# Sums by heads on quarters of the array, partial sums for z, constants made on chip, and the last units in halves

## The chip, the cores and the metric

The kernel runs on one core of a Trainium2 chip. The metric is the device time of one execution in microseconds. Below, PE is TensorE (the 128x128 matmul array), DVE is VectorE, ACT is ScalarE, POOL is GpSimd and SP is SyncE, whose queue issues every DMA of this kernel.

## What is computed

A linear attention with a quadratic feature map, followed by a feed-forward net with a depthwise convolution of three taps and a gate. Batch is 4, heads 4, sequence 1088, head size 32, r is 8, d_ff is 1024.

```python
def phi(x):
    a = np.einsum('rd,bhsd->bhsr', S1, x)
    b = np.einsum('rd,bhsd->bhsr', S2, x)
    return np.einsum('bhsi,bhsj->bhsij', a, b).reshape(*x.shape[:-1], r * r)
q_p, k_p = phi(q), phi(k)
kv = np.einsum('bhsf,bhsd->bhfd', k_p, v)
z = np.sum(k_p, axis=2)
num = np.einsum('bhsf,bhfd->bhsd', q_p, kv)
den = np.einsum('bhsf,bhf->bhs', q_p, z)[..., None] + 1e-06
x = num / den                       # then heads side by side: B, S, 128
...
h = np.maximum(x @ w_in, 0.0)
conv_out = sum(conv_w[k] * hp[:, k:k + S, :] for k in range(3))   # hp: h with a zero row at both ends
gate = 1.0 / (1.0 + np.exp(-conv_out))
out = (h * gate) @ w_out
```

## The kernel before

**Small matrices.** S1, S2, the taps, w_in and w_out come as float64 and are turned into float32 on chip from their two 32-bit words (`to_f32`, steps low, e, m, clamp, f, power, sign, value). `sab` holds S1 and S2 of all four heads as a block diagonal, 64 columns. A further load `pk` (80 KB, tile `pks`) brings the 128x128 identity that every transpose needs, and `zmask`, the block mask of z. `s2t` transposes the S2 half of `sab`.

**Attention, k side**, for each batch b, in three groups g of three chunks of 128 positions. `k_ab` multiplies k by `sab` (a and b of all heads in 64 columns), `k_take` copies them to SBUF, `k_phi` makes the outer products (256 columns: 4 heads by 64 features) on DVE or POOL by `kphi`. `k_kv` sums v by features over nine chunks; it works with two heads a matmul: two matmuls of 64 array columns each, at array columns 0 and 64, both with 128 moving columns, of which only the blocks of the own head are used (`k_kvmask`). With "J" in `kvs` the nine chunks are summed in one go, with "S" group by group. `k_kvt` transposes the sum, `k_kvtake` copies it. For z the kernel doesn't sum features: `k_z` sums b times a over the positions as a 32x32 matrix on array columns 0 to 31, `k_zmask` keeps the blocks, and `k_wz` folds it with S2 into 32 extra columns of the weights by which q is multiplied (`k_wq`).

**Attention, q side**, for each batch and group: `q_ab` (a, b and the part for the denominator, 96 columns), `q_take`, `q_ac`, `q_sum`, `q_rec`, `q_div` (the quotient is taken into a). Then one of two ways by `qside`: with "T", `q_phi` makes the outer product, six PE transposes (`q_t`) turn it and ACT copies it (`q_ttake`); with "M", `q_turn` transposes the small a and b on DVE, `q_out` writes them to DRAM with four DMAs, `q_in` reads them back as repeated rows with six, and `q_phi` multiplies the rows (on DVE or POOL by `qphi`). `q_x` multiplies by the sums of batch b, on two halves of the array, and `q_hi` and `q_lo` store x as a rounded part and a rest.

**Feed-forward.** The positions of all batches stand in one row, cut into nine segments (382, seven of 510, and 404 columns). A unit is a segment and one of eight blocks of 128 hidden channels, 72 in all. Its steps are `f_in` (three matmul passes: rounded weights and rests), `f_relu` on ACT, `f_mid` (the middle tap, on ACT or DVE by `mid`), two taps on DVE, `f_gate` (sigmoid, ACT), `f_mul` on POOL (on DVE for the last unit, `late`), and `f_out` (two passes of a float32 matmul, summed over eight units in one PSUM bank). Then `f_store` (DVE) and `f_send` (DMA).

**The order of the work.** Nothing in the kernel loops in this order. `graph` lists all steps with a cost, what they wait for, the PSUM banks and buffers they hold, and a key; `schedule` plays them against models of the engines and returns one order in which every engine's queue is filled. The keys come from `CFG` (`F0`, `P`, `kdue`, `kstep`, `kvlag`, `qlead`, ...), and `loads` is the order of the input DMAs. PSUM has eight banks: four for f_in ("u"), one for the output sums ("o") and three for all the rest ("t"); a "t" step may also take a free "u" bank until the time `share`. Matmuls on a constant tile (`fill`, L512) stand in early gaps of PE.

The lines that the prediction speaks of: L512 `fill`, L592 `wqs`, L599 `s2t`, L612 `outer`, L628 `k_ab`, L646 `k_z`, L667 `k_kv`, L724 `q_turn`, L752 `q_phi` by rows, L766 `q_t`, L777 `q_x`, L825 to L827 `f_in`, L844 `f_mid` on DVE, L848 taps, L856 `f_gate`, L863 `f_mul`, L887 `f_out`, L892 `f_store`.

Of the kernel before, what the change touches and what calls it, by code (L numbers as in the profile page):

```python
# [9 lines left out]
F32 = mybir.dt.float32  # L10
# [9 lines left out]
P = 128  # L20
# [26 lines left out]
C_ID = 0  # L47
C_ZM = C_ID + P
C_END = C_ZM + HR

# [12 lines left out]
    "loads": "s k0.2 t k0.0 q0.1 k0.1 q0.0 c i1 q0.2 i0 o0 v0 i3 k1 o2 o1 k2 i2 v1 o3 v2 q2 v3 q3 k3 q1",  # L63

    "F0": 108819.35,
    "P": 2174.27,
    "wlead": -80468.59,
    "outlag": 5.18,
    "tapa": 6055.15,
    "tkey": -87094.92,  # L70

    "kdue": [59700.0, -192994.0, -123572.0, 87470.0],
    "kstep": [-4098.0, 47885.0, -31405.0, 47192.0],
    "kvlag": -40175.81,

    "qlead": [[-31940.0, 61515.0, -68231.0], [131916.0, 73634.0, 73287.0], [35879.0, -31506.0, 43322.0], [4524.0, -170059.0, -45604.0]],
# [9 lines left out]
    "stick": -20253.84,  # L86
# [12 lines left out]
ALT = {"qside": "TM", "kvs": "SJ", "fr": "FR", "mid": "AD"}  # L99
POOLS = {"u": 4, "o": 1, "t": 3, "h": 6, "s": 3, "g": 6, "f": 3, "w": 3, "kab": 6, "kp": 8, "qs": 3, "gh": 3, "os": 2, "kv": 2, "qr": 2, "qf": 2, "d": 2}  # L100
BEGIN = {"PE": 5900.0, "ACT": 3000.0, "DVE": 1800.0, "POOL": 1400.0, "SP": 29500.0}
KB = {"s": 64, "t": 25, "c": 82, "k": 557, "v": 590, "q": 557, "i": 262, "o": 262}
# [5 lines left out]
COLD = 6400.0  # L108
# [32 lines left out]

def cut(n, i, half):
    return (0, n) if not half else (0, n // 2) if i == 0 else (n // 2, n)


def graph(cfg):
# [14 lines left out]
    issue, done = 730.0, 0.0  # L161
    for name in cfg["loads"].split():
        kb = KB[name[0]] / (NG if "." in name else 1)
        issue += 430
        before, done = done, max(issue + 1400, done) + kb / (0.242 if done < 10800 else 0.413)
        landed["dma", name] = done + 60
# [14 lines left out]
    ev("wqs", c_pool(B * W_S, 1.0), [("s", "value")], key=-4e4)  # L181
    ev("s2t", c_pe(60), [("s", "value"), ("dma", "c")], [("s2ps", "t")], key=-4e4)
# [34 lines left out]
    for b in range(B):  # L217
        due, ks, lag = cfg["kdue"][b], cfg["kstep"][b], cfg["kvlag"]
        for g in range(NG):
# [5 lines left out]
            if cfg["kvs"][0][b] == "J":  # L225
                if g == NG - 1:
                    kps = [("kp", b, i) for i in range(NG)]
                    deps = [x for i in range(NG) for x in (("k_phi", b, i), dma("v", b, i))]
                    ev(("k_kv", b, g), c_pe(NG * 654 + 152, 75), deps, [(kv, "t")], [kv, *kps], key + lag)
                continue  # L230
            ev(
                ("k_kv", b, g),
                c_pe(806, 75),
# [7 lines left out]
        ev(("k_z", b), c_pe(685, 65), [("k_take", b, g) for g in range(NG)], [(("zps", b), "t")], abs_, key)  # L241
        ev(("k_zmask", b), c_dve(32), [("k_z", b), ("dma", "c")], uses=[("zps", b)], key=key)
# [6 lines left out]
        for g in range(NG):  # L249
# [28 lines left out]
            ev(("q_x", b, g), c_pe(1.667 * NT[g] + 156, 70), deps, [(x, "t")], uses, key)  # L278
            ev(("q_hi", b, g), c_act(NT[g]), [("q_x", b, g)], uses=[x], key=key)
            ev(("q_lo", b, g), c_dve(NT[g]), [("q_hi", b, g)], uses=[x], key=key)  # L280

    for u in range(NU):
# [3 lines left out]
        a, o = ("a", u), ("o", s)  # L286
# [7 lines left out]
        ev(("f_in", u), c_pe(3 * (n + 2) / 2.4 + 62, 225), [*x, ("i", j, "rest")], [(a, "u")], key=key)  # L294
        half = u >= NU - cfg["halves"]
        out, prior = key + cfg["outlag"] * step, [("f_out", u - 1, i) for i in parts(cfg, u - 1)] if u else []
        for i in parts(cfg, u):
            new = i == 0
            m = cut(n, i, half)
            m = m[1] - m[0]  # L300
            ev(("f_relu", u, i), c_act(m + 2), [("f_in", u)], [(("h", u), "h")] if new else [], [a, ("h", u)], soon)
            deps = [("f_relu", u, k) for k in range(i + 1)] + [("t", "value")]
            mid = c_act(m, 1) if cfg["mid"][s][f] == "A" else c_dve(m, 1)
            ev(("f_mid", u, i), mid, deps, uses=[a, ("h", u)], key=soon)
            ev(("f_tapa", u, i), c_dve(m, 1), [("f_mid", u, i)], uses=[a, ("h", u)], key=soon + cfg["tapa"])
            ev(("f_tapb", u, i), c_dve(m, 1), [("f_tapa", u, i)], uses=[a, ("h", u)], key=soon)
            ev(("f_gate", u, i), c_act(m), [("f_tapb", u, i)], [(("s", u), "s")] if new else [], [a, ("s", u)], soon)
            mul = c_dve(m, lock=True) if u >= NU - cfg["late"] else c_pool(m)
            ev(("f_mul", u, i), mul, [("f_gate", u, i)], [(("g", u), "g")] if new else [], [("h", u), ("s", u), ("g", u)], soon)
            first = [] if f or i else [(o, "o")]  # L310
            if cfg["fr"][s][f] == "R":
                ev(("f_high", u, i), c_act(m), [("f_mul", u, i)], [(("gh", u), "gh")] if new else [], [("g", u), ("gh", u)], soon)
                ev(("f_low", u, i), c_pool(m), [("f_high", u, i)], uses=[("g", u), ("gh", u)], key=soon)
                deps = [("f_low", u, i), ("o", j, "rest"), *prior]
                ev(("f_out", u, i), c_pe(3 * m / 2.4 + 62, 225), deps, first, [o, ("g", u), ("gh", u)], out)
            else:
                deps = [("f_mul", u, i), ("o", j, "value"), *prior]
                ev(("f_out", u, i), c_pe(4 * m / 2.4 + 5, 160), deps, first, [o, ("g", u)], out)
            if f == NF - 1:
                ev(("f_store", s, i), c_dve(m), [("f_out", u, i)], [(("os", s, i), "os")], [o], soon)  # L320
                ev(("f_send", s, i), c_dma(1, 1400), [("f_store", s, i)], uses=[("os", s, i)], key=soon)
# [3 lines left out]
def schedule(cfg):  # L325
# [11 lines left out]
    def pool(kind):  # L337
        if kind == "t" and now["PE"] < cfg["share"] and pools["u"] and pools["u"][0] < (pools["t"] or [(1e9, 0)])[0]:
            return pools["u"]
        return pools[kind]  # L340
    after = collections.defaultdict(list)
# [25 lines left out]
    for _ in range(len(events)):  # L367
        best = None
        for e in ("PE", "ACT", "DVE", "POOL", "SP"):
            able = []  # L370
            for name in waiting[e]:
                cost, _, alloc, key = events[name]
                t = max(now[e], ready[name])
                if not all(pool(kind_of[b]) for b in alloc):
                    continue
                for b in alloc:
                    t = max(t, pool(kind_of[b])[0][0])
# [10 lines left out]
        for b in alloc:  # L388
            slot[b] = heapq.heappop(pool(kind_of[b]))[1]
# [21 lines left out]
def body(ctx: ExitStack, tc: tile.TileContext, qT, kT, v, pk, ps, pt, w_in, w_out, outT):  # L411
# [41 lines left out]
    ptr = const.tile([P, 2 * W_T], I32, name="ptr")  # L453
    pks = const.tile([P, C_END], F32, name="pks")
    for name in CFG["loads"].split():
# [6 lines left out]
            "c": lambda: e.dma_start(pks, pk),  # L462
# [7 lines left out]
    ident = pks[:, C_ID : C_ID + P]  # L470
    kmask = const.tile([P, P], F32, name="kmask")
    zmask = pks[:HR, C_ZM : C_ZM + HR]
    sab = const.tile([P, W_S], F32, name="sab")
    pts = const.tile([P, W_T], F32, name="pts")
    s2b = const.tile([HR, P], F32, name="s2b")
# [93 lines left out]
    to_f32(("t",), pts, ptr, True)  # L569
# [21 lines left out]
    def wqs():  # L591
        nc.gpsimd.tensor_copy(wq[:, :, : 2 * HR], sab.unsqueeze(1).broadcast_to([P, B, 2 * HR]))  # L592
# [8 lines left out]
    def s2take():  # L601
        nc.scalar.copy(s2b, do["s2ps"][:HR, :P])
# [360 lines left out]
```

## Time and profile before

| | |
|---|---|
| median of 3 runs | 165.84 us (165.67 to 166.76) |
| the profiled execution | 166.0 us |
| its span | 164.2 us |
| PE busy | 156.4 us (95%), 823 matmuls |
| DVE busy | 147.0 us (89%) |
| ACT busy | 133.7 us (81%) |
| POOL busy | 123.2 us (75%) |
| granted PE clock | 1.00 in every slice |
| DMA | 20.34 MB, mean 124 GB/s |

The span runs from the first to the last instruction of the program; the execution's own time is a little longer. Busy times are unions of the instructions' durations on an engine. A matmul's duration holds its drain, which overlaps with the matmuls that follow, so the mean duration of one is longer than what it adds to the queue; that is read from the distance of starts. "Idle before" is the time that an engine stood still ahead of an instruction, and the releaser is what ended it.

### The profile page before, as it was taken

To read this page: it belongs to the slowest core of one execution; us is meant where nothing else is said; L and a number is where in the kernel's file an instruction comes from. 1 tells how busy PE (TensorE), PEld (TensorE's weight loads), DVE (VectorE), ACT (ScalarE), POOL (GpSimd) and SP (SyncE) were. 2 spreads that over 40 slices of the span, in tenths; PEclk is the share of its full clock that TensorE was granted. 3 is DMA by queue.
4 is the path that set the end of the run, shared out by engine and by line. 5 is a ranking of instruction groups with operands and counts; after the bars stand their busy time and mean duration, and the time that the engine had idled before them with its cause. 6 is when DMAs were issued, how large, how long until landed. Compare 5 with 4: busy or idle time off the path is not lost.

```text
span 164.2 us, 2830 instructions
## 1 busy us (share of the span) xinstructions
PE 156.4 (95%) x823; PEld 102.9 (63%) x823; DVE 147.0 (89%) x304; ACT 133.7 (81%) x284; POOL 123.2 (75%) x120
## 2 busy tenths in 40 slices
PE   7699999999999999999999999999999999999981
PEld 7588989888766756446444654664565556556620
DVE  4469999889897999999999999999999999999971
ACT  4133755649897999998998999999899998999950
POOL 3403999933997699697996769998877787779760
PEclk9999999999999999999999999999999999999999
DMA  4999999024644643545544453300100100200101
GB/s 105 264 281 411 409 411 346 23 69 106 175 97 140 198 116 98 152 140 164 158 115 133 129 168 119 115 0 0 64 0 0 68 0 0 67 2 0 64 0 50
DMA packets 19711, 20.34 MB, mean 124 GB/s; under 512 B 9712, under 2 KB 17392, under 8 KB 19696
## 3 DMA queue, kind: packets, MB, share of 16 engines
q1 hardware_dynamic: 19696, 20.17, 38.8%
q8 instruction: 6, 0.10, 0.3%
q14 instruction: 9, 0.07, 0.1%
HBM read 16.95 MB, written 3.21 MB: 123 GB/s over the span
## 4 chain that ended last, share of the span: by engine, by line
PE 74%; DMA 17%; SPq 3%; issue 2%; POOL 1%; POOLq 1%; DVE 0%
PE o L887 34%; DMA kt<-in_kT 12%; PE a L825 10%; PE a L826 9%; PE a L827 9%; PE t L777 5%; PE t L694 4%; DMA qt<-in_qT 3%; DMA w_out_raw<-d 2%; POOL g L863 1%; PE t L667 1%; PE t L628 1%; SPq L463 1%; POOLq L930 1%; SPq L464 1%
## 5 line engine op out<-in xcount | busy, mean ns | idle before, releaser
L863 POOL TENSOR_TENSOR g<-h,s 128x510 f32<-128x510 f32 (+2 forms) x71 | 87.2, 1246 | 20.0 <-ACT s L856 18.9
L848 DVE SCALAR_TENSOR_TENSOR a<-h,pts,a 128x510 f32<-128x510 f32 (+2 forms) x144 | 98.6, 720 | 4.0 <-ACT a L842 2.5
L887 PE MATMUL o<-g,w_out_sb 128*128 128x510 f32 (+2 forms) x144 | 70.7, 577 | 0.6 <-POOL g L863 0.6
L825 PE MATMUL a<-xhi,whi 128*128 128x512 f32 (+2 forms) x72 | 48.9, 679 | 0.0
L842 ACT ACTIVATE a<-h,pts 128x510 f32<-128x510 f32 (+2 forms) x67 | 45.0, 676 | 0.6
L836 ACT ACTIVATE h<-a 128x512 f32<-128x512 f32 (+2 forms) x72 | 41.5, 578 | 3.7 <-PE a L827 3.3
L856 ACT ACTIVATE s<-a 128x510 f32<-128x510 f32 (+2 forms) x72 | 41.6, 579 | 1.5 <-DVE a L848 1.4
L887 PEld LDWEIGHTS o<-g,w_out_sb 128*128 128x128 f32 x144 | 26.0, 189 | 12.0 <-POOL g L863 4.8
L826 PE MATMUL a<-xhi,wlo 128*128 128x512 f32 (+2 forms) x72 | 27.7, 384 | 0.0
L827 PE MATMUL a<-xlo,whi 128*128 128x512 f32 (+2 forms) x72 | 27.6, 384 | 0.0
L825 PEld LDWEIGHTS a<-xhi,whi 128*128 128x128 f32 x72 | 13.6, 189 | 17.8 <-ACT s L856 6.2
L826 PEld LDWEIGHTS a<-xhi,wlo 128*128 128x128 f32 x72 | 13.7, 190 | 11.4 <-issue 10.2
L827 PEld LDWEIGHTS a<-xlo,whi 128*128 128x128 f32 x72 | 13.5, 188 | 2.4
L612 POOL TENSOR_TENSOR kp<-kab 128x768 f32<-128x768 f32 x8 | 11.9, 1512 | 4.0 <-ACT kab L632 4.0
L632 ACT COPY kab<-t 128x192 f32<-128x192 f32 x12 | 3.8, 319 | 7.8 <-PE t L628 7.7
L694 PEld LDWEIGHTS t<-wq,qt 128*128 128x128 f32 x72 | 8.9, 191 | 1.5 <-ACT qab L698 0.6
L628 PE MATMUL t<-sab,kt 128*128 128x64 f32 x72 | 9.2, 274 | 0.6 <-DMA kt<-in_kT 0.6
L628 PEld LDWEIGHTS t<-sab,kt 128*128 128x128 f32 x72 | 8.7, 192 | 1.2 <-ACT f L526 0.5
L694 PE MATMUL t<-wq,qt 128*128 128x96 f32 x72 | 9.2, 275 | 0.0
L667 PE MATMUL t<-kp,vt 128*64 128x128 f32 x144 | 8.5, 275 | 0.4 <-DMA vt<-in_v 0.4
L667 PEld LDWEIGHTS t<-kp,vt 128*64 128x64 f32 x144 | 7.8, 137 | 1.0 <-DMA vt<-in_v 0.6
L612 DVE TENSOR_TENSOR kp<-kab,t 128x768 f32<-128x768 f32 x4 | 3.8, 954 | 4.0 <-ACT kab L632 4.0
(86 smaller groups left out, 142.5 us busy)
## 6 DMA issues: line engine op xcount, KB each, us to landing
vt<-in_v SPq DMA_DIRECT2D x4, 576.0 KB
w_in_raw<-d SPq DMA_DIRECT2D x10, 192.0 KB
w_in_raw<-d SPq DMA_DIRECT2D x20, 96.0 KB
w_out_raw<-d SPq DMA_DIRECT2D x10, 192.0 KB
w_out_raw<-d SPq DMA_DIRECT2D x20, 96.0 KB
kt<-in_kT SPq DMA_DIRECT2D x3, 544.0 KB
qt<-in_qT SPq DMA_DIRECT2D x3, 544.0 KB
w_in_raw<-in_w_in SPq DMA_DIRECT2D x4, 256.0 KB
```

The costliest lines, as they stand in the source:

```text
L628: nc.tensor.matmul(pv[:, :, j, :], kt[:, b, c * P : (c + 1) * P], sab, start=True, stop=True)
L667: nc.tensor.matmul(ps[64 * pr : 64 * (pr + 1), :P], vt[:, b, c, 64 * pr : 64 * (pr + 1)], st["kp", g][:, j, P * pr : P * (pr + 1)], start= ...
L694: nc.tensor.matmul(pv[:, :, j, :], qt[:, b, c * P : (c + 1) * P], wq[:, b], start=True, stop=True)
L825: nc.tensor.matmul(a[:, : n + 2], whi[:, w], xhi[:, x], start=True, stop=False)
L826: nc.tensor.matmul(a[:, : n + 2], wlo[:, w], xhi[:, x], start=False, stop=False)
L827: nc.tensor.matmul(a[:, : n + 2], whi[:, w], xlo[:, x], start=False, stop=True)
L836: nc.scalar.activation(st["h"][:, c], a[:, c], AF.Relu)
L842: nc.scalar.activation(st["a"][:, lo:hi], h, AF.Copy, scale=cw[:, f, 1:2])
L848: nc.vector.scalar_tensor_tensor(out=a, in0=h[:, lo + k : hi + k], scalar=cw[:, f, k : k + 1], in1=a, op0=ALU.mult, op1=ALU.add)
L856: nc.scalar.activation(st["s"][:, c], st["a"][:, c], AF.Sigmoid)
L863: e.tensor_tensor(out=st["g"][:, lo:hi], in0=st["h"][:, lo + 1 : hi + 1], in1=st["s"][:, lo:hi], op=ALU.mult)
L887: nc.tensor.matmul(o, w_out_sb[:, w], st["g"][:, c], start=first, stop=final)
```

## The change

- `k_kv` takes one head a matmul: four matmuls of 32 array columns a chunk, at array columns 0, 32, 64 and 96, with the 64 moving columns of the own head. `k_kvmask` reads the same 64 columns twice and masks as before. Batches 1 and 3 are summed group by group ("S"), 0 and 2 in one go.
- `k_z` puts chunk c on the quarter c % 4, so that four partial sums stand below each other; `k_zmask` works on 128 partitions, and `k_wz` sums them, since S2 now stands four times below itself (`s24`, copied on POOL in `wqs`, and a full 128x128 transpose in `s2t`, which waits for `wqs`).
- The load `pk` is gone. POOL makes the identity with a memset and an `affine_select`; `zmask` comes with the taps.
- The last three units are worked in halves of 202 columns from `f_in` on, the second half's in a bank of its own, and the output of the last segment is summed, stored and sent in two halves with a bank each.
- `q_x` may be done for two groups at once (`xs`: batches 0 and 2 groups 0 and 1, batch 1 groups 1 and 2, batch 3 one by one).
- `q_in` has four row buffers in place of two.
- `schedule` has other costs and keys, and the order of all work is drawn up anew from them. Among the choices: loads of batch 0's k in one piece and of batch 1's k ahead of batch 0's v; `mid` has nine units on DVE in place of five; the `q_phi` by rows are all on POOL (three were on DVE); batch 1's group 0 takes the way "T" in place of "M"; `kphi` has four on DVE as before, one in each batch.

```diff
-    "loads": "s k0.2 t k0.0 q0.1 k0.1 q0.0 c i1 q0.2 i0 o0 v0 i3 k1 o2 o1 k2 i2 v1 o3 v2 q2 v3 q3 k3 q1",
+    "loads": "s k0 q0.0 t q0.1 i0 k1 q0.2 v0 o1 k2 o0 i2 i1 v1 o2 o3 q2 q1 v2 i3 v3 k3 q3",
...
-    "kphi": ["DDP", "PPP", "PDP", "DPP"],
-    "qphi": ["DPP", "PPD", "PDP", "DPP"],
+    "kphi": ["PPD", "PPD", "PPD", "PPD"],
+    "qphi": ["DPP", "PPP", "PPP", "PPP"],
-    "qside": ["TTM", "MMM", "MMM", "MMM"],
-    "kvs": ["JJJJ"],
+    "qside": ["TTM", "TMM", "MMM", "MMM"],
+    "kvs": ["JSJS"],
+    "xs": ["QPQS"],
...
-    "mid": ["AAAAAAAA", "AAAAAAAA", "AAAAADAA", "AAAAAAAA", "AAAAAAAA", "AADAADAA", "AADAAAAA", "ADAAAAAA", "AAAAAAAA"],
+    "mid": ["AAAAAAAA", "DAAAAAAA", "AAAAAADA", "ADAAAAAD", "AAADAAAD", "AADAAAAA", "AADAAAAA", "AAAAAAAA", "ADAAAAAA"],
-    "halves": 0,
+    "halves": 3,
-    "share": 74099.86,
+    "share": 160744.4,
...
+GROUPS = {"S": [[0], [1], [2]], "J": [[0, 1, 2]], "P": [[0], [1, 2]], "Q": [[0, 1], [2]]}
...
+        nc.gpsimd.memset(ident, 0.0)
+        nc.gpsimd.affine_select(ident, ident, [[-1, P]], ALU.not_equal, 1.0, base=0, channel_multiplier=1)
...
     def wqs():
+        nc.gpsimd.tensor_copy(s24.rearrange("p (t r) -> p t r", r=HR), sab[:, HR:].unsqueeze(1).broadcast_to([P, P // HR, HR]))
         nc.gpsimd.tensor_copy(wq[:, :, : 2 * HR], sab.unsqueeze(1).broadcast_to([P, B, 2 * HR]))
...
-        nc.tensor.transpose(ps[:HR, :P], sab[:, HR:], ident)
+        nc.tensor.transpose(ps[:, :P], s24, ident)
...
-                nc.tensor.matmul(ps[:HR, :HR], ab[:, 1, j, :], ab[:, 0, j, :], start=c == 0, stop=c == NCH - 1)
+                t = HR * (c % 4)
+                o = ps[t : t + HR, :HR]
+                nc.tensor.matmul(o, ab[:, 1, j, :], ab[:, 0, j, :], start=c < 4, stop=c + 4 >= NCH, tile_position=(0, t))
...
-                for pr in range(2):
+                for h in range(H):
                     nc.tensor.matmul(
-                        ps[64 * pr : 64 * (pr + 1), :P],
-                        vt[:, b, c, 64 * pr : 64 * (pr + 1)],
-                        st["kp", g][:, j, P * pr : P * (pr + 1)],
+                        ps[D * h : D * (h + 1), :RR],
+                        vt[:, b, c, D * h : D * (h + 1)],
+                        st["kp", g][:, j, RR * h : RR * (h + 1)],
                         start=c == 0,
                         stop=c == NCH - 1,
-                        tile_position=(0, 64 * pr),
+                        tile_position=(0, D * h),
                     )
...
-            nc.vector.tensor_tensor(out=kvm, in0=st["kvps"][:, :P], in1=kmask, op=ALU.mult)
+            a, b = (x.rearrange("p (h r) -> p h r", h=2) for x in (kvm, kmask))
+            nc.vector.tensor_tensor(out=a, in0=st["kvps"][:, :RR].unsqueeze(1).broadcast_to([P, 2, RR]), in1=b, op=ALU.mult)
...
-        def q_x(g):
+        def q_x(last):
+            for g in next(x for x in GROUPS[CFG["xs"][0][b]] if last in x):
+                x_of(g)
...
+        half, split = len(parts(CFG, u)) > 1, len(outs(CFG, u)) > 1
+
+        def f_in(i):
+            st["a", i] = a = bank(("a", u, i), "t" if i else "u", "a")
+            lo, hi = cut(n, i, half)
+            c, w = slice(lo + 2 * i, hi + 2), slice(f * P, (f + 1) * P)
+            x = slice(OFF[g] + lo + 2 * i, OFF[g] + hi + 2)
+            nc.tensor.matmul(a[:, c], whi[:, w], xhi[:, x], start=True, stop=False)
+            nc.tensor.matmul(a[:, c], wlo[:, w], xhi[:, x], start=False, stop=False)
+            nc.tensor.matmul(a[:, c], whi[:, w], xlo[:, x], start=False, stop=True)
...
         def f_out(i):
-            c, w = slice(*cut(n, i, half)), slice(f * P, (f + 1) * P)
-            if f == 0 and i == 0:
-                acc[g] = bank(("o", g), "o", "o")
-            o, first, final = acc[g][:, c], f == 0, f == NF - 1 and i == parts(CFG, u)[-1]
+            c, w = slice(*cut(n, i, split)), slice(f * P, (f + 1) * P)
+            if f == 0:
+                acc[g, i] = bank(("o", g, i), "t" if i else "o", "o")
+            o, first, final = acc[g, i][:, c], f == 0, f == NF - 1
```

More of the change, by code (lines that the diff above doesn't have):

```diff
@@ L92 @@
     "late": 1,
-    "halves": 0,
+    "halves": 3,
     "fills": 22000.0,
-    "share": 74099.86,
+    "share": 160744.4,
 }
[L99 to L102, printed above, removed]
+ALT = {"qside": "TM", "kvs": "SJ", "fr": "FR", "mid": "AD", "xs": "SJPQ"}
@@ L139, in parts, with outs @@
     return range(2 if u >= NU - cfg["halves"] else 1)
+def outs(cfg, u):
+    return range(2 if cfg["halves"] and u >= NU - NF else 1)
 def cut(n, i, half):
@@ L293, in graph @@
         j = f * P // CVT
-        ev(("f_in", u), c_pe(3 * (n + 2) / 2.4 + 62, 225), [*x, ("i", j, "rest")], [(a, "u")], key=key)
-        half = u >= NU - cfg["halves"]
-        out, prior = key + cfg["outlag"] * step, [("f_out", u - 1, i) for i in parts(cfg, u - 1)] if u else []
+        half = len(parts(cfg, u)) > 1
+        h, g, gate, gh = ("h", u), ("g", u), ("s", u), ("gh", u)
         for i in parts(cfg, u):
-            new = i == 0
-            m = cut(n, i, half)
+            m, a = cut(n, i, half), ("a", u, i)
@@ L303, in graph @@
             mid = c_act(m, 1) if cfg["mid"][s][f] == "A" else c_dve(m, 1)
[L304 to L307, printed above, removed]
+            ev(("f_mid", u, i), mid, deps, uses=[a, h], key=soon + i)
@@ L310, in graph @@
-            first = [] if f or i else [(o, "o")]
+            ev(("f_mul", u, i), mul, [("f_gate", u, i), *[("f_mul", u, k) for k in range(i)]], [] if i else [(g, "g")], [h, gate, g], soon + i)
             if cfg["fr"][s][f] == "R":
[L312 to L315, printed above, removed]
-            else:
-                deps = [("f_mul", u, i), ("o", j, "value"), *prior]
-                ev(("f_out", u, i), c_pe(4 * m / 2.4 + 5, 160), deps, first, [o, ("g", u)], out)
+                ev(("f_high", u, i), c_act(m), [("f_mul", u, i), *[("f_high", u, k) for k in range(i)]], [] if i else [(gh, "gh")], [g, gh], soon + i)
+                ev(("f_low", u, i), c_pool(m), [("f_high", u, i)], uses=[g, gh], key=soon + i)
```

183 lines of the change are left out of this document (110 added, 73 removed).

## The prediction

> **What bounds the kernel now.** I read the split of the span into stretches first, which says which engine never rests where. Its columns are the stretch in us, its length, then the busy us and the instructions of PE, PEld (weight loads), DVE, ACT and POOL, the granted clock, the DMA share and GB/s.
>
> ```profile
> 4.90:14.24 9.34, 7.05 (x67) 6.23 (x66) 5.38 (x15) 3.56 (x13) 1.51 (x1) 1.00 0.94 296
> 14.24:155.20 140.96, 140.44 (x725) 91.19 (x726) 134.67 (x266) 125.31 (x263) 116.41 (x95) 1.00 0.37 118
> 155.20:164.20 9.00, 4.95 (x13) 1.60 (x11) 4.27 (x7) 2.87 (x7) 3.32 (x4) 1.00 0.06 23
> 60.00:150.00 90.00, 89.83 (x298) 50.69 (x297) 87.90 (x140) 86.36 (x165) 75.75 (x59) 1.00 0.26 79
> ```
>
> TensorE (PE) works 140.44 of the 140.96 us between 14.24 and 155.20: this stretch is as long as its list of matmuls. Ahead of it lies a start with 2.29 us of PE idle, behind it a tail of 9.00 us. DVE is close behind, at 134.67 of 140.96 (95.5%), and 97.7% from 60 to 150 (87.90 of 90); it will matter as soon as PE has less to do.
>
> The chain of waits (start, us, what), in the middle of the feed-forward units, says what a visit to a tiled array costs:
>
> ```profile
> 59.59 0.85 PE o L887 x2
> 60.44 0.80 PE t L777 x4
> 61.24 0.43 PE a L825
> ...
> 62.14 0.85 PE o L887 x2
> 62.99 0.24 PE a L825
> ```
>
> Two passes of 510 columns take 0.85, so 0.833 ns a column. q_x (L777) streams 384 columns in two passes on two halves at once, 0.64 by that rate, but takes 0.80, and the next f_in starts with 0.43 in place of 0.24: about 0.35 us for going there and back.
>
> **The sums by heads.** All of k_kv (L667) and two batches of k_z (L646) in the timeline (start, us, engine, line):
>
> ```profile
> 14.24 2.19 PE L667 MATMUL t<-kp,vt 128*64 128x128 f32 x36 [0.40 <-DMA vt<-in_v]
> 24.86 4.15 PE L667 MATMUL t<-kp,vt 128*64 128x128 f32 x72
> 39.13 2.19 PE L667 MATMUL t<-kp,vt 128*64 128x128 f32 x36
> 21.33 1.33 PE L646 MATMUL t<-kab 128*32 128x32 f32 x36
> ```
>
> and one batch of k_kv in slices of 10 ns (the count is of matmuls in flight, then of weight loads):
>
> ```profile
> 14.72:14.73 0.01, 0.01 (x5) 0.01 (x2) 1.00 2.10 845
> 14.73:14.74 0.01, 0.01 (x6) 0.01 (x4) 1.00 1.05 410
> 14.83:14.84 0.01, 0.01 (x5) 0.01 (x3) 1.00 2.10 819
> 14.84:14.85 0.01, 0.01 (x6) 0.01 (x4) 1.00 0.00 0
> ```
>
> In neighbouring slices two matmuls and two weight loads start, one for each half, and the next pair 0.11 us later. The step is 128 columns at 0.833 (0.107) and 3 ns. So tiles of different columns run beside each other, loads included; 18 pair-steps of 0.11 make 1.98 us a batch. Now four quarters start together and stream 64 columns: a step of 0.053 + 0.003, 18 of them, 1.01. That is 0.97 less a batch, 3.9 us in four, if four tiles do what two do. k_z goes from one tile to four: now 1.33/36, at most 37 ns an instruction and in the run about 31 (its last one's drain aside); on four tiles, between 7 or so (the offset that slices of 10 ns allow) and 31. I take 8, as the nearest row is that of the tiles that start together: 18 times 23 ns is 0.41 a batch, 1.25 us for the three batches that lie in the full stretch. The other end for both is no gain, or a loss, and is a rival below.
>
> **What is put back on PE.** The new split of k_kv in batches 1 and 3 into three pieces adds four visits, the joined q_x of batches 0, 1 and 2 take three away: between 3 x 0.35 saved and 1 x 0.35 lost, as pieces may stand beside other tiled work; I take 0.3 saved. Group 0 of batch 1 no longer goes through DRAM but through six transposes:
>
> ```profile
> 18.54 0.82 PE L766 MATMUL t<-pks,kp 128*128 128x128 f32 x6
> L752 DVE TENSOR_TENSOR w_out_raw<-w_out_raw 128x768 f32<-128x768 f32 x2 | 1.9, 952 | 0.0
> L752 DVE TENSOR_TENSOR w_in_raw<-w_in_raw 128x768 f32<-128x768 f32 x1 | 1.1, 1131 | 0.0
> L724 DVE STREAM_TRANSPOSE qr<-qab 128x192 f32<-128x192 f32 x10 | 3.7, 371 | 0.0
> L844 DVE TENSOR_SCALAR a<-h,pts 128x510 f32<-128x510 f32 x5 | 3.7, 747 | 0.0
> L752 POOL TENSOR_TENSOR w_in_raw<-w_in_raw 128x768 f32<-128x768 f32 x4 | 7.3, 1831 | 0.0
> PEld o L887 <- POOL g L863: 4.8, 8, 0.9
> ```
>
> That is +0.7 (0.82 less the overlap with what follows). PE in the full stretch: -3.9 - 1.25 - 0.3 + 0.7 = -4.75, so 136.2 of 140.96.
>
> **What holds next: DVE.** The three q_phi rows leave DVE (1.9 + 1.1), one q_turn goes (0.37), and four more f_mid come to it (4 x 0.747 = 2.99): 134.67 - 3.37 + 2.99 = 134.3. At the 97.7% that it reaches from 60 to 150 with PE full beside it, 134.3 us of work need 137.4. So I take 3.5 us off the stretch, not 4.75. ACT loses the four f_mid and gains two copies; at 125.31 it isn't near. POOL takes three q_phi of 1.83 (5.5 us): 116.41 + 5.5 is 122 of 137, 89%. Each stands ahead of the f_mul queued behind it, for which f_out on PE waits. I cost this at nothing, because g has six buffers and f_out comes some five units after its f_in, which hides it; with that cover gone, PE waits up to 0.9 each (the longest wait for POOL in the last row), 2.7 us.
>
> The group that turns to transposes also takes its ten DMAs (four out, six in) out of SP's queue, and two more qf buffers let later q_in start sooner; PE has no gap worth naming in the full stretch in which it would wait for rows (0.52 in all), so both count nothing.
>
> **The start.** In the timeline of PE, and of POOL, with two rows of the DMA issues:
>
> ```profile
> 8.46 0.28 PE L599 MATMUL t<-pks,sab 128*32 128x128 f32 x1 [1.59 <-DMA pks<-in_pk]
> 9.20 0.66 PE L512 MATMUL warm<-idle 128*128 128x128 f32 x4
> 10.48 0.49 PE L512 MATMUL warm<-idle 128*128 128x128 f32 x2
> 11.23 0.49 PE L512 MATMUL warm<-idle 128*128 128x128 f32 x2
> 4.23 0.40 POOL L592 COPY wq<-sab 128x256 f32<-128x256 f32 x1 [1.94 <-DVE sab L563]
> 6.13 1.51 POOL L612 TENSOR_TENSOR kp<-kab 128x768 f32<-128x768 f32 x1 [1.50 <-ACT kab L632]
> kt<-in_kT SPq DMA_DIRECT2D x3, 544.0 KB
> kt<-in_kT SPq DMA_DIRECT2D x1, 160.0 KB
> ```
>
> s2t waits 1.59 us for the constants, with a k_ab queued behind it; the identity now made on POOL ends that. Idle (2.29) and fillers (1.64) are 3.9 us of the 9.34, and the stretch ends when v of batch 0 lands (0.40 at 14.24 above). The new load order puts k of batch 1 ahead of that v, so k_ab can fill the gap, and longer rows in place of k's three parts; but the first k_ab now needs all of k of batch 0. Between 0.5 lost (544 KB in place of the first part's 160) and 3.9 gained, I take 1.6, the wait that is removed. The POOL work is free: memset and select fall into the 1.94 idle, the copy of S2 (128 columns, about 0.2 by the 0.40 for 256) into the 1.50; uncovered, 0.2 to 0.7 on the first k_phi. s2t's wait for that copy has k_ab behind it on PE, and the copy is done by about 5. kmask, zmask and the wider k_zmask change no count or length worth a tenth.
>
> **The tail.** ACT, DVE and the chain's last steps:
>
> ```profile
> 152.79 5.62 DVE L848 SCALAR_TENSOR_TENSOR a<-h,pts,a 128x404 f32<-128x404 f32 x9
> 158.50 0.51 ACT L856 ACTIVATE s<-a 128x404 f32<-128x404 f32 x1 [0.81 <-DVE a L848]
> 159.04 0.58 DVE L863 TENSOR_TENSOR g<-h,s 128x404 f32<-128x404 f32 x1 [0.63 <-ACT s L856]
> 158.86 1.77 PE o L887 x4
> 160.66 0.58 DVE L892 COPY o<-o 128x404 f32<-128x404 f32 x1 [1.04 <-PE o L887]
> L892 DVE COPY o<-o 128x510 f32<-128x510 f32 x7 | 4.8, 682 | 0.0
> L848 DVE SCALAR_TENSOR_TENSOR a<-h,pts,a 128x510 f32<-128x510 f32 x112 | 79.6, 747 | 2.5 <-ACT a L842 1.5
> ```
>
> By 510 against 404, a copy is 0.58 for 404 and about 0.37 for 202. Gate, mul, out and store of the last half save 0.17 + 0.21 + 0.34 + 0.21 = 0.9 behind the last tap, and a smaller last store up to 0.5. Against it, DVE taps run without a gap for 5.62 us, and six more of them, each with some 0.2 that a half doesn't shrink (0.747 at 510, 0.624 at 404 in the run), are 1.2. On PE the halves add nine f_in passes and sixteen f_out passes, which fall into its 4.05 idle us there. Between -1.4 and +1.2; I take -0.2.
>
> **The sum.** -3.5 - 1.6 - 0.2 = -5.3 on a span of 164.2: 158.9. The profiled execution took 166.0, 1.8 above its span, so 160.7; the median of the runs is 0.16 below that execution, so 160.5 us.
>
> **The rivals.** (A) The forecast: 158.2 to 162.5, chance 0.55. (B) DVE holds more: its queue is strict, and its share of the stretch stays at 95.5%. 134.3/0.955 = 140.6, only 0.4 off the stretch; with start and tail 2.2 in all, 163.6. For it speaks that 134.3 us hardly change; against it, that DVE's gaps shrink to 2.3% wherever PE is full. Chance 0.22, most of it below 164.2. (C) Slower: quarters cost their instructions. Twice as many instructions run in k_kv, and no row shows weight loads and matmuls of a run closer than k_z's 31 ns on the mean, except in pairs. At 31 ns 72 of them take 2.23, +0.25 a batch, +1.0 in all; k_z gains nothing; all four visits cost (+1.4), the joins return 1.0, the transposes 0.7: +2.1, the start returns 0.8, the tail costs 0.6: 167.7. If they took turns altogether (72 x 0.056 = 4.0) it would be near 174. It decides from 27.5 ns an instruction on. Against it stand the pairs that start within 10 ns. Chance 0.12. The Trainium skill has a rule for this side, in "TensorE: Matmul & The Clock Gate", section "Wait — 56ns, not 53.3ns?": start to start never drops below about 25 ns however few columns there are. By that k_kv would be an estimated 1.8 us a batch and gain 0.7 in all, not 3.9. In this trace the pairs break that floor, since they stand in neighbouring slices of 10 ns; for four tiles no run here shows it. (D) Better: the start gives 3.0, the tail 1.0, and PE's whole 4.75 counts: 157.1; chance 0.11.
>
> **How the numbers follow.** A difference under 1% (164.2 to 167.5) can't be told from none. Faster: 0.55 + 0.11 + 0.14 of B = 0.80; same: 0.08 of B and 0.05 of C = 0.13; slower: 0.07. The range 157.6 to 164.6 holds A, half of D and nearly all of B, about 0.8.
>
> **What would show it.** In the changed profile k_kv should be about 1.2 us a batch (x72) and k_z about 0.4 to span; over 2.1 and C is right. The full stretch should begin near 12.6 without a wait of s2t for DMA, and be 137 to 138 us long, with DVE at 97% of it; PE idle put down to DVE, ACT or POOL in it would mean B. Behind the last tap there should be some 4.8 us in place of 5.8. If k_ab waits for DMA beyond 6 us, or f_out for POOL more than 4.8 us in total, the start or the moved q_phi was costed wrongly.

## The result and the profile after

The median of the changed kernel is 159.75 us over four executions, against 166.22 us for the kernel before in four: a ratio of 0.960 (95% interval 0.954 to 0.965). In a second session, `after_again` below, it was 0.964 (0.959 to 0.969). The forecast was 160.5, range 157.6 to 164.6. One execution of the changed kernel, at 164.79 us, ran under a half-rate PE clock for 10 us near its start; the profile read here is the one of 160.22 us (span 158.4, granted clock 1.00), and all ratios and comparisons leave such executions out.

The rows of that profile's split into stretches, with the columns as in the prediction:

```profile
10.27:155.20 144.93, 144.02 (x933) 94.84 (x933) 140.53 (x289) 129.87 (x282) 122.93 (x103) 1.00 0.36 114
60.00:150.00 90.00, 90.00 (x317) 52.55 (x315) 88.34 (x141) 86.52 (x169) 79.39 (x62) 1.00 0.21 63
```

PE is still the engine that never rests, with 0.91 us idle in 144.93. DVE now stands at 97.0% of this stretch (140.53/144.93; 95.5% before), and in the feed-forward units from 60 to 150 us three engines are within 4% of each other: PE 100%, DVE 98.2%, ACT 96.1%.

The timeline of PE in the same profile (start, us, engine, line), where k_z is L695, k_kv L717, k_wz L703, q_x L834 and q_t L819:

```profile
9.05 0.38 PE L695 MATMUL t<-kab 128*32 128x32 f32 x18
10.27 0.41 PE L703 MATMUL t<-zt,s2b 128*128 128x32 f32 x2 [0.43 <-DVE zt L699]
11.00 1.55 PE L745 MATMUL t<-wq,qt 128*128 128x96 f32 x12
15.16 1.21 PE L717 MATMUL t<-kp,vt 128*32 128x64 f32 x72
20.33 0.54 PE L717 MATMUL t<-kp,vt 128*32 128x64 f32 x24
23.54 1.51 PE L834 MATMUL t<-kp,kv 128*64 128x384 f32 x8
25.88 1.38 PE L717 MATMUL t<-kp,vt 128*32 128x64 f32 x72
```

A batch of k_kv in one go takes 1.21 where it took 2.19, though it has twice as many instructions (batch 2, at 25.88, takes 1.38, as its first three matmuls start 0.08 to 0.1 us apart); a batch in three pieces takes 3 x 0.54; k_z takes 0.38 where one batch took 0.76. The groups of both lines, over all four batches (they stood at 8.5 and 2.8 us before):

```profile
L717 PE MATMUL t<-kp,vt 128*32 128x64 f32 x288 | 5.8, 222 | 0.1
L695 PE MATMUL t<-kab 128*32 128x32 f32 x72 | 1.5, 199 | 0.0
```

Where the time went can be read from marks that both traces have. k_kv of batch 0, with k_ab of two batches, k_z and all q_ab of batch 0 ahead of it, is done at 16.37 here; in the kernel before the last of the same work (k_ab of batch 1) is done at 18.59. The first f_in pass of the 17th unit starts at 57.63 (before 62.54), of the 61st at 132.99 (137.95); the last tap ends at 154.01 (158.41), the span at 158.4 (164.2). So 2.2 us are won by the first mark, 4.9 by the second, nothing between the second and third, and the tail adds 0.8. The marks don't part the work quite alike: at the second one the changed kernel still has 6 matmuls of q_ab and 4 of q_x ahead that the kernel before had done (about 1.5 us by distances from start to start), and at the third the f_out of one more unit (0.85).

Up to the 61st unit I also added up, for each step, the distances from one matmul's start to the next one's, which counts the idle time behind it too. k_kv lost 3.2 us (8.35 to 5.18), k_z 1.4 (2.63 to 1.24), k_kvt and k_wz 1.1 together, and q_x 0.4; q_t gained 1.5 (12 transposes to 18). k_ab lost 2.2 and the fillers gained 2.0: the kernel waits as long for its first loads as before, with matmuls on a constant tile in place of gaps.

The tail in the timelines of DVE and of ACT (L906 is the taps, L921 f_mul, L950 f_store, L945 f_out, L914 f_gate):

```profile
149.09 4.92 DVE L906 SCALAR_TENSOR_TENSOR a<-h,pts,a 128x404 f32<-128x404 f32 x13
153.92 0.86 DVE L921 TENSOR_TENSOR g<-h,s 128x202 f32<-128x202 f32 x2
155.00 0.86 DVE L950 COPY o<-o 128x202 f32<-128x202 f32 x2 [0.21 <-PE o L945]
```

```profile
154.04 0.34 ACT L914 ACTIVATE s<-a 128x202 f32<-128x202 f32 x1 [0.40 <-DVE a L906]
```

Behind the last tap there are 4.4 us (158.4 - 154.01) in place of 5.8, and the store that waited 1.04 us for f_out now waits 0.21.

### The profile page after: what moved, and what is told of

The parts are those of the page before. It is cut to its first block, busy times and chain, and to the rows that moved or that the text cites. A ratio compares the mean times of both kernels' runs of the same rounds, so it can differ in the third digit from the quotient of the medians.

```text
span 162.9 us, 3185 instructions
## 1 busy us (share of the span) xinstructions
PE 156.6 (96%) x1000; PEld 107.0 (66%) x1000; DVE 145.4 (89%) x312; ACT 133.3 (82%) x291; POOL 127.6 (78%) x128
## 4 chain that ended last, share of the span: by engine, by line
PE 75%; DVE 9%; POOL 5%; DMA 4%; ACT 3%; issue 1%; SPq 1%
PE o L945 34%; PE a L885 9%; PE a L886 9%; PE a L887 9%; DMA w_in_raw<-in_w_in 4%; PE t L674 4%; PE t L745 4%; PE t L834 4%; POOL g L921 3%; POOL kp L658 2%; PE t L717 2%; DVE f L589 1%; DVE w L602 1%; DVE a L906 1%; PE t L819 1%
## 5 line engine op out<-in xcount | busy, mean ns | idle before, releaser
L906 DVE SCALAR_TENSOR_TENSOR a<-h,pts,a 128x510 f32<-128x510 f32 (+3 forms) x150 | 99.1, 699 | 1.7 <-ACT a L900 0.2
L921 POOL TENSOR_TENSOR g<-h,s 128x510 f32<-128x510 f32 (+3 forms) x73 | 85.9, 1196 | 14.9 <-ACT s L914 10.3
L945 PE MATMUL o<-g,w_out_sb 128*128 128x510 f32 (+2 forms) x160 | 70.3, 533 | 0.1
L885 PE MATMUL a<-xhi,whi 128*128 128x512 f32 (+4 forms) x75 | 48.8, 651 | 0.0
L894 ACT ACTIVATE h<-a 128x512 f32<-128x512 f32 (+3 forms) x75 | 42.5, 574 | 4.2 <-PE a L887 3.7
L900 ACT ACTIVATE a<-h,pts 128x510 f32<-128x510 f32 (+3 forms) x66 | 43.9, 667 | 0.6
L914 ACT ACTIVATE s<-a 128x510 f32<-128x510 f32 (+3 forms) x75 | 42.4, 570 | 1.1 <-DVE a L906 0.7
L945 PEld LDWEIGHTS o<-g,w_out_sb 128*128 128x128 f32 x160 | 28.5, 189 | 7.2 <-POOL g L921 1.5
L886 PE MATMUL a<-xhi,wlo 128*128 128x512 f32 (+4 forms) x75 | 28.2, 377 | 0.0
L887 PE MATMUL a<-xlo,whi 128*128 128x512 f32 (+4 forms) x75 | 28.2, 376 | 0.0
L902 DVE TENSOR_SCALAR a<-h,pts 128x510 f32<-128x510 f32 (+1 forms) x9 | 6.6, 733 | 1.0 <-ACT h L894 1.0
L717 PE MATMUL t<-kp,vt 128*32 128x64 f32 x288 | 6.7, 245 | 0.1
```

Source lines behind the costliest of these rows:

```text
L885: nc.tensor.matmul(a[:, c], whi[:, w], xhi[:, x], start=True, stop=False)
L886: nc.tensor.matmul(a[:, c], wlo[:, w], xhi[:, x], start=False, stop=False)
L887: nc.tensor.matmul(a[:, c], whi[:, w], xlo[:, x], start=False, stop=True)
L894: nc.scalar.activation(st["h"][:, c], a[:, c], AF.Relu)
L900: nc.scalar.activation(st["a", i][:, lo:hi], h, AF.Copy, scale=cw[:, f, 1:2])
L906: nc.vector.scalar_tensor_tensor(out=a, in0=h[:, lo + k : hi + k], scalar=cw[:, f, k : k + 1], in1=a, op0=ALU.mult, op1=ALU.add)
```

## The experiments

Each ratio is to the kernel before on the same chip in the same session, and microseconds between two kernels are given by their medians and by their ratios, at 165.5 us for 1. The 95% intervals of the ratios reach 0.4 to 0.9% to each side (0.7 to 1.5 us), so that a difference of about a microsecond between two kernels can hardly be told from none.

**The changed kernel again**, as the base of the others.

> The changed kernel once more, unaltered, for its time beside the experiments and for a profile in which the granted clock stays at 1.00. By the first profile's half clock from 11.2 to 21.2 us (span 162.9 there, 157.1 to 158.0 in the other executions) I expect 159.5 us, the first f_in near 28 us in place of 32.67, and k_kv at 1.3 us a batch.

Ratio 0.964 (0.959 to 0.969), a median of 159.9 us against 165.5. The gain stands, at 5.7 us.

**k_kv on halves again**, all else as changed, the order too.

```diff
-                for h in range(H):
+                for pr in range(2):
                     nc.tensor.matmul(
-                        ps[D * h : D * (h + 1), :RR], ...
+                        ps[64 * pr : 64 * (pr + 1), :P], ...
```

> k_kv goes back to two heads a matmul on halves (k_kvmask too); order, banks and all else stay as changed. Theory 1 (PE's list of matmuls sets the time up to the tail, and quarters shorten it): a batch takes 2.0 us again in place of 1.05, so 3.1 to 3.9 us more than the changed kernel. Rival (the new order, the loads and the start made the gain, DVE bounds now): less than 1 us more.

163.08 us, ratio 0.985 (0.981 to 0.989): 3.2 us slower than the changed kernel of the same session by the medians, 3.5 by the ratios. Its group in PE's list:

```profile
L717 PE MATMUL t<-kp,vt 128*64 128x128 f32 x144 | 9.6, 278 | 0.0
```

So 9.6 - 5.8 = 3.8 us of PE became 3.2 us of time. In the order of the changed kernel, nearly all of what the quarters save on PE arrives, and no other single part that was undone below costs as much.

**k_z in one sum**, all else as changed.

```diff
-                t = HR * (c % 4)
-                o = ps[t : t + HR, :HR]
-                nc.tensor.matmul(o, ab[:, 1, j, :], ab[:, 0, j, :], start=c < 4, stop=c + 4 >= NCH, tile_position=(0, t))
+                nc.tensor.matmul(ps[:HR, :HR], ab[:, 1, j, :], ab[:, 0, j, :], start=c == 0, stop=c == NCH - 1)
```

> k_z goes back to one 32x32 tile (with k_zmask and k_wz on 32 partitions); order and all else stay as changed. Theory 1: 0.3 to 0.4 us a batch on PE, 0.9 to 1.6 us more in all. Rival (another engine hides it): within 0.5 us of the changed kernel.

160.66 us, ratio 0.971 (0.967 to 0.975): 0.8 us more than the changed kernel by the medians, 1.2 by the ratios, whose intervals overlap. k_z takes 3.0 us in it against 1.5. That agrees with the four partial sums being worth about what they save, but it is hardly clear of the noise.

**Quarters alone in the old kernel**: k_kv and k_kvmask of the change in the kernel before, with its order, loads and everything else.

> The kernel before with k_kv on quarters alone (and k_kvmask on the 64 columns), in the order of before. Theory 1 (quarters shorten PE's list in a stretch that is gapless): 2.5 to 3.9 us less than before. Rival (it needs the new order, as DVE and POOL hold the early stretch): within 1 us of before.

Ratio 0.997 (0.993 to 1.002): 0.4 us, no difference that can be told, though k_kv does shrink. PE's timeline of this kernel (k_kv is L667, k_kvt L683, k_ab L628):

```profile
24.64 2.55 PE L667 MATMUL t<-kp,vt 128*32 128x64 f32 x144
27.44 0.33 PE L683 MATMUL t<-pks,kvm 128*128 128x128 f32 x1 [0.26 <-DVE kvm L679]
28.56 0.85 PE L628 MATMUL t<-sab,kt 128*128 128x64 f32 x6 [0.79 <-DMA kt<-in_kT]
```

Two batches take 2.55 where they took 4.15, and k_kvt then waits 0.26 for the mask on DVE and k_ab 0.79 for a load of k, where the kernel before waits 0.35 (at 29.61). Of the 1.6 us freed here at least 0.7 go into these two waits; in this profile the first f_in starts 0.83 us sooner than in the kernel before (35.16 against 35.99). That PE's list alone sets the time fell here, as 2.5 us lie far outside the interval; the rival, that the quarters need an order to suit, is what the run agrees with.

**The same with k of batch 3 loaded earlier**, to see whether that load was all that kept the gain back.

```diff
-    "loads": "... o3 v2 q2 v3 q3 k3 q1",
+    "loads": "... o3 v2 k3 q1 q2 v3 q3",
```

> The kernel before with quarters in k_kv, as in e_before_kv4, and the load of batch 3's k issued ahead of batch 3's v (and q of batch 1 after it) in place of near the end; order of the engines as before. Theory 3 (in the old order PE's freed time went into waiting for that load): the 0.79 us wait for k at 28.5 us goes, the first f_in starts 1.9 us sooner than in the kernel before (0.8 with the quarters alone), the time falls 1.5 to 2.5 us below before. Rival (DVE and POOL hold the early stretch): first f_in and time as in e_before_kv4, within 0.5 us.

Ratio 1.001 (0.997 to 1.005), no gain either. The load's wait is gone, and PE waits for DVE in its place:

```profile
29.30 0.33 PE L683 MATMUL t<-pks,kvm 128*128 128x128 f32 x1 [0.33 <-DVE kvm L679]
31.29 0.33 PE L683 MATMUL t<-pks,kvm 128*128 128x128 f32 x1 [1.03 <-DVE kvm L679]
```

and the split of its span from 24 to 36 us, where the kernel with the old loads has 11.17 us of DVE and 10.11 of POOL, and the kernel before 10.86 and 9.79:

```profile
24.00:36.00 12.00, 10.61 (x213) 8.57 (x210) 11.43 (x38) 7.11 (x23) 11.77 (x14) 1.00 0.40 143
```

This profiled execution began late under a lower granted clock (0.82 from 12 to 24 us), so its rows show where PE waits and not how long, and its stretch from 24 to 36 us doesn't hold quite the same work as the others'. They point at DVE and POOL as what holds the k side in the old order, with the load beside it; that is not shown, and no run settles the shares. Taken with the halves above: by the ratios, all the rest of the change without quarters is worth 1.5% (2.5 us), the quarters without the rest 0.3% (0.4 us), both 3.6% (6.0 us). The gains don't add, and which part of the rest lets the quarters count (the order of the work, the q_phi that left DVE, or another) wasn't taken apart.

**More work on PE**: twenty units, every third from 9 to 66, get one f_in pass twice.

```diff
+            if u in plus:
+                nc.tensor.matmul(a[:, c], whi[:, w], xhi[:, x], start=True, stop=True)
             nc.tensor.matmul(a[:, c], whi[:, w], xhi[:, x], start=True, stop=False)
```

> In 20 units (every third of 8 to 67) the first pass of f_in is issued twice (0.23 us each on PE, 4.7 us in all, the same result); nothing else changes. If PE's list sets the time: 3.7 to 4.7 us more than the changed kernel. If DVE or ACT sets it and PE has room: under 2 us more.

Ratio 0.987 (0.978 to 0.996): 3.8 us more than the changed kernel by the ratios, 3.5 by the medians, for some 4.7 us of work.

**More work on DVE**: the same units get a copy of 96 columns ahead of their first tap.

```diff
+            if u in plus and k == 0:
+                nc.vector.tensor_copy(scratch[:, :96], a[:, :96])
```

> In the same 20 units DVE copies 96 columns of the unit's bank to an unused tile ahead of the first tap (about 0.25 us each, 5 us in all); nothing else changes. Theory 1, as the prediction has it (DVE right behind PE, at its ceiling): 2.5 to 5 us more. Rival (PE alone sets the time, DVE's idle takes it up): under 1.5 us more.

Ratio 0.985 (0.978 to 0.993): 3.6 us more. The added group and the stretch of the units:

```profile
L909 DVE COPY scratch<-a 128x96 f32<-128x96 f32 x20 | 5.0, 252 | 0.1
```

```profile
60.00:150.00 90.00, 88.90 (x301) 49.82 (x299) 88.60 (x152) 84.43 (x160) 76.72 (x60) 1.00 0.20 60
```

PE, full in the changed kernel, now rests 1.1 us in 90. So work on DVE costs nearly what work on PE costs (3.6 of 5.0, 3.5 to 3.8 of 4.7, with some 1.5 us of uncertainty on each): both are the bound. The profiles say the same: from the first f_in pass of the 17th unit to the end of the last tap 96.4 us pass in the changed kernel, 100.0 with the work on PE and 100.1 with that on DVE. Each added piece also lengthens the way of its unit from engine to engine, in an order drawn up without it, and no run separates that from the engine being full.

**More work on ACT**: the same units get a copy of 220 columns ahead of their gate.

```diff
+            if u in plus:
+                nc.scalar.copy(scratch[:, :220], st["a", i][:, :220])
```

> In the same 20 units ACT copies 220 columns of the unit's bank to an unused tile ahead of f_gate (about 0.24 us each, 4.7 us in all); nothing else changes. The prediction took ACT as far from the bound: under 1.5 us more. If ACT is as close as DVE: 2.5 to 5 us.

Ratio 0.977 (0.970 to 0.983): 1.9 us by the medians, 2.2 by the ratios, between the two expectations. The copies' own records add up to 7.4 us, but they overlap with their neighbours', and ACT's busy time in all grew by 4.1 (133.4 to 137.5). About half of that reaches the end (in the profile 98.6 us from the 17th unit to the last tap, against 96.4). That looks like less than on DVE, but the intervals overlap: ACT isn't far from the bound.

**f_mid as before**: five units on DVE in place of nine, all else as changed, the order too.

```diff
-            if CFG["mid"][g][f] == "A":
+            if MID_BEFORE[g][f] == "A":
                 nc.scalar...
```

`MID_BEFORE` stands for the list of the kernel before. It moves more than four units: seven of the nine go back to ACT, and three others come to DVE.

> f_mid on DVE for the five units of the kernel before in place of the nine of the changed one, order otherwise as changed: DVE has 2.9 us less, ACT 2.4 us more. By what the added work cost (5.0 us on DVE cost some 3.5, 4.7 us on ACT some 2), I expect 0.5 to 1 us less than the changed kernel. Rival (the order was drawn up for these places, ACT's steps come late at their new ones): the same or up to 1 us more.

161.3 us, ratio 0.974 (0.967 to 0.981): 1.4 us slower by the medians, 1.7 by the ratios, although DVE has four f_mid, some 3 us, less to do. I had expected a gain, and the loss is larger than the rival had it. Two rows of its waits, and the row of the changed kernel that answers to the first:

```profile
DVE a L906 <- ACT a L900: 4.3, 8, 1.5
PEld o L945 <- POOL g L921: 2.8, 4, 0.9
```

```profile
DVE a L906 <- ACT a L900: 0.5, 2, 0.3
```

The taps now wait 4.3 us for f_mid on ACT, 0.5 in the changed kernel. So in this order the new places of f_mid pay, which the forecast had only as a cost of 2.99 us to DVE. Whether the larger number on DVE does, or only that the order was drawn up for these places, the run doesn't separate.

**The last units whole.**

```diff
-    "halves": 3,
+    "halves": 0,
```

> The last three units whole again, one bank and one store for the last segment; the rest of the order as changed. The prediction gave the halves 0.2 us (between 1.4 gained and 1.2 lost). By the traces, behind the last tap there are 4.4 us now against 5.8 before, so I expect 0.5 to 1.2 us more than the changed kernel. Rival (the halves' extra instructions eat it): within 0.3 us of the changed kernel.

161.33 us, ratio 0.974 (0.967 to 0.982): 1.5 us slower by the medians, 1.8 by the ratios, where the intervals are 1.3 us and 0.8 us to each side. It is more than expected. The span of its profile is 848.5 us, which no row of the others can be set beside, so none shows where.

**k_zmask of batch 0 right behind its k_z.** In the changed kernel the start's chain of waits is this:

```profile
3.07 6.61 DMA w_in_raw<-in_w_in
...
9.70 0.43 DVE em L580
10.13 0.10 DVE zt L699
...
10.27 0.41 PE t L703 x2
```

and DVE's timeline there:

```profile
9.70 0.43 DVE L580 TENSOR_SCALAR em<-w_in_raw 128x256 int32<-128x256 int32 x1 [1.08 <-DMA w_in_raw<-in_w_in]
10.04 0.18 DVE L699 TENSOR_TENSOR zt<-t,ptr 128x32 f32<-128x32 f32 x1
```

k_zmask (L699, 0.18) stands in DVE's queue behind the first step of w_in's conversion (L580), which waits 1.08 us for its load, though k_z is done at 9.43; k_wz on PE waits for k_zmask, and q_ab for k_wz. The edit takes it ahead:

```diff
+    order = list(order)
+    order.remove(("k_zmask", 0))
+    order.insert(order.index(("k_z", 0)) + 1, ("k_zmask", 0))
```

> In DVE's queue k_zmask of batch 0 stands ahead of the first step of w_in's conversion, which waits until 9.71 us for its load; nothing else moves. Theory 2 (that load's wait holds k_zmask, k_wz on PE and all of q behind it): k_wz starts near 8.9 in place of 10.28 us, PE's 1.47 us idle falls under 0.3, the time falls by 0.7 to 1.4 us, and the clock doesn't drop. Rival (the start is bound by the loads of k and v that follow): PE idles elsewhere in the start instead, time within 0.4 us of the changed kernel.

160.15 us, ratio 0.968 (0.963 to 0.972): no gain, as the rival had it. PE's timeline of it:

```profile
9.40 0.41 PE L703 MATMUL t<-zt,s2b 128*128 128x32 f32 x2
18.86 0.52 PE L819 MATMUL t<-ident,kp 128*128 128x128 f32 x3 [0.84 <-DVE qd L762]
27.91 0.43 PE L885 MATMUL a<-xhi,whi 128*128 128x384 f32 x1
```

k_wz comes 0.87 us earlier (9.40 against 10.27), and 0.84 of that is lost again at 18.86 to a wait for q_rec on DVE; the first f_in starts at 27.91 against 27.97. So PE's gap at the start is not what bounds there; the next wait, which takes the gain up, is one for DVE.

**The same with four more fillers** ahead of k_wz, so that PE doesn't rest there in any execution.

> As e_zt_first (k_zmask of batch 0 ahead of the conversion in DVE's queue), and four more matmuls on a constant tile on PE ahead of k_wz, where the first profile of the changed kernel shows 1.47 us of idle and half the clock behind it. If PE's idle there brings the half clock, no execution has a mean clock under 0.98, and the time stays within 0.5 us of the changed kernel's. If the drop has another cause, some executions still have it.

160.9 us, ratio 0.972 (0.965 to 0.978): 1.0 us slower than the changed kernel by the medians, 1.3 by the ratios, where 0.5 was expected at most; the intervals overlap. In its profile k_wz starts at 10.86, later than in the changed kernel (10.27), so the fillers more than fill the gap. Its mean granted clock was 0.997 or more in each of seven executions.

## Why the prediction was right, step by step

**The quarters.** Predicted 0.97 us a batch: measured 2.19 - 1.21 = 0.98. That four tiles do what two did is seen in slices of 10 ns of one batch (as in the prediction, counts are of matmuls in flight, then of weight loads):

```profile
15.28:15.29 0.01, 0.01 (x8) 0.01 (x9) 1.00 0.00 0
15.29:15.30 0.01, 0.01 (x9) 0.01 (x9) 1.00 0.53 205
15.30:15.31 0.01, 0.01 (x11) 0.01 (x9) 1.00 0.53 205
15.31:15.32 0.01, 0.01 (x12) 0.01 (x9) 1.00 0.00 0
15.35:15.36 0.01, 0.01 (x14) 0.01 (x10) 1.00 0.00 0
```

Four more matmuls are in flight within four slices, and the next ones join 0.05 to 0.06 us on: the step of 64 columns (0.056) that was forecast. On the mean one starts every (1.21 - 0.222)/71 = 13.9 ns. Rival C needed 31 ns and decided from 27.5 on, so it is out, and putting the halves back cost 3.2 us, within the 3.1 to 3.9 expected. The rule of the Trainium skill ("TensorE: Matmul & The Clock Gate", section "Wait — 56ns, not 53.3ns?") that starts never come closer than about 25 ns doesn't hold in this trace for matmuls on different columns of the array, at 13.9 ns on the mean.

**z.** Predicted 0.41 a batch: 0.76 to 0.38 in the batch shown, 1.3 us over all four by busy time (2.8 to 1.5).

**What is put back on PE** was mis-sized, each term by less than a microsecond. Splitting batches 1 and 3 costs more than the joins return: k_kv saves 2.7 us by busy time and 3.2 by distances from start to start, not 3.9, as a split batch takes 3 x 0.54 = 1.62 where a joined one takes 1.21 (without the last drains 3 x 0.47 and 1.03). A joined q_x takes 1.51 where two single ones take 0.87 each, drains included, and all joins together saved 0.4, not 3 x 0.35. So the visits cost some 0.3 net where I had 0.3 saved. The six transposes cost 1.5 by distances, idle time among them, not 0.7. Against that stand 1.1 us less in k_kvt and k_wz, which I hadn't counted.

**DVE as the next bound.** Right as a mechanism: 97.0% of the stretch, and the added work shows it. The cut that I derived from it, 4.75 down to 3.5, isn't confirmed. From the first mark to the 61st unit 4.96 - 2.2 = 2.8 us were won, with 1.4 more in the first mark that are k_kv and k_z of batch 0 (0.98 + 0.38): 4.1 in all, between the two numbers, or 3.3 if the f_out that now stands behind the mark (0.85) is counted here. So the marks can't decide between 3.5 and 4.75. That the units between the second and third mark won nothing says nothing of DVE either: all k_kv and k_z are done before the 17th unit in both kernels, so no shortened matmul stands there. The sign that the full stretch would begin near 12.6 and be 137 to 138 us long didn't come. PE is almost without idle from 10.27 to 155.20, but it has 144.01 us of work in the same stretch of the kernel before too (144.02 now), so the length of that stretch doesn't show where time was won. The step "this stretch is as long as its list of matmuls" was incomplete: with the quarters in the old order PE's list is shorter and the time hardly is. It is true only with the rest of the change beside it, which the forecast took for granted. Rival B (DVE's share stays at 95.5%) is out; what it describes is nearer to the kernel of the quarters alone, where DVE stands at 96.2% between 14.24 and 155.20 (135.65 of 140.96) and PE's idle there grows from 0.52 to 1.87.

**ACT "isn't near"** was too light: ACT is busy for 96.1% of the units' time, and 4.1 us more of it cost about 2.

**The start** was forecast at 1.6 us. s2t's wait is gone, as said, and k_ab waits for no DMA beyond 6 us. But of the 2.2 us at the first mark 1.36 are k_kv and k_z, so the start gave 0.85. What took the rest is the place of k_zmask, which the forecast held to be worth less than a tenth: its length is, its place in DVE's queue behind a load is not. With it moved, k_kv of batch 0 starts 0.87 us sooner (14.29 against 15.16). But moving it also showed that these 0.87 us bring nothing to the whole.

**The tail** was forecast at -0.2: 0.9 to 1.4 saved behind the last tap against 1.2 for six more taps. The saving is 1.4. The taps cost less: twelve of 202 columns are busy 4.3 us, and six of 404 were 6 x 10.0/16 = 3.75. That makes -0.8, with 4.4 us behind the last tap where some 4.8 were forecast. Without halves the kernel is 1.5 to 1.8 slower, with an interval that reaches down to about 0.2. Between 0.8 and 1.8 it stays open.

**POOL's three more q_phi** cost nothing that shows, as said: f_out waits for POOL 1.5 us in all, less than before (4.8).

```profile
PEld o L945 <- POOL g L921: 1.5, 3, 0.9
```

**The sum.** Forecast -3.5 - 1.6 - 0.2 = -5.3 of span; measured -4.1 - 0.85 - 0.8 = -5.8 (164.2 to 158.4), or -3.3 for the stretch and -1.7 for the tail if that f_out is counted with the stretch. By the first count the stretch and the tail gave some 0.6 more each, the start 0.75 less. That the sum comes so close is partly luck, as these misses cancel in part, and so do those inside the stretch. What was right is the gain of the quarters, by the mechanism forecast; how much this gain needs the rest of the change was not foreseen.

## What to carry to other kernels

A matmul that uses a part of the array's columns can have its neighbours run beside it on the others, and then, as here, the streamed columns count and not the instructions: sum by tile what streams, and read the offset between tiles from slices of 10 ns rather than from the mean of one tile's run. When an engine is full and a second one is 2 to 5% behind it, work taken off the first may be worth little until the rest of the kernel follows: undo the one part, and also do it alone, since the two differ (3.2 us and 0.4 here). Where a queue is worked off in order, the place of a short instruction can count for more than its length (0.87 us against 0.18 here): look at what stands ahead of it and what that waits for. And look at what comes next before moving it, since here the next wait took all of it up.

## What the runs showed of the hardware

Matmuls on four different column tiles start some 7 ns apart (four within the slices above), weight loads with them, and one starts every 13.9 ns on the mean, in float32 with 64 streamed columns.

In the profile of the execution of 164.79 us the same gap at k_wz is longer, since the load of w_in lands no earlier (k_zmask at 10.05 against 10.04) and PE is done with k_z sooner (8.40 against 9.43). PE's timeline and the split into stretches:

```profile
10.28 0.41 PE L703 MATMUL t<-zt,s2b 128*128 128x32 f32 x2 [1.47 <-DVE zt L699]
11.01 2.69 PE L745 MATMUL t<-wq,qt 128*128 128x96 f32 x12
```

```profile
11.00:11.50 0.50, 0.49 (x3) 0.50 (x4) 0.07 (x1) 0.37 (x1) 0.00 (x0) 0.69 1.05 424
11.50:12.00 0.50, 0.50 (x4) 0.50 (x4) 0.49 (x2) 0.00 (x0) 0.00 (x0) 0.50 1.00 413
21.00:21.50 0.50, 0.50 (x14) 0.44 (x5) 0.26 (x2) 0.00 (x0) 0.00 (x0) 0.57 1.00 386
```

The columns are those of the split above. PE rests 1.47 us, and about 1 us later the granted clock falls to 0.50 and stays there until some 21.4 us, with PE busy all the while. The Trainium skill ("TensorE: Matmul & The Clock Gate", section "What's actually happening") has the half rate follow an idle window of about 3.4 us and end after about as long of work; here less than half of that idle went ahead of it, and it lasted 10 us. That the gap is the cause is not shown. For it speaks that with fillers in it none of seven executions showed a mean clock under 0.997. Against it, as the sole cause, stand two other profiles: the kernel before rests 1.59 us ahead of s2t and keeps a clock of 1.00, and the kernel of the quarters with k of batch 3 loaded earlier rests only 0.74 us there (at 8.47), but then has a clock of 0.50 from about 9.4 to 16.2 us. So the length of the gap alone doesn't decide, and what does stays open.
